# Scores and values on column tiles of their own, softmax groups of two heads and an earlier start, in a two-part attention decode kernel

## The chip, the cores and the metric

One core of one Trainium2 chip. The metric is the device time in microseconds (us), the median of the fast runs. The kernel before takes 1594.34 us (15 runs, 1592.09 to 1597.1).

## The reference

One decode step (one query token) of two attention blocks, their outputs side by side (shortened):

```python
# x (1,1,512); wq (512, 4096); wo (4096, 512); all bfloat16
def _A_ref(x, k_cache, v_cache, wq, wo):              # 32 heads, 32768 keys each
    q = (x @ wq) -> (1, 32, 1, 128)
    scores = einsum("bhqd,bhkd->bhqk", q, k_cache) * (128 ** -0.5)
    o = einsum("bhqk,bhkd->bhqd", softmax(scores), v_cache)
    return o.reshape(1, 1, 4096) @ wo
# _B_ref: the same with 8 KV heads for 32 query heads, and only the last 4096 keys
return concatenate([a, b], axis=-1)
```

Block A's caches are 32 x 32768 x 128 x 2 bytes, 268 MB each for K and V; with B and the weights, 570 MB have to be read. There is almost no reuse.

## The kernel before

A *chunk* is 1024 tokens of one KV head (1056 of them). TensorE (PE) transposes a chunk's K (called K below), multiplies it with the query (S, scores), and after the softmax multiplies the probabilities with V (PV). The code is shortened.

```python
NK_SLOTS = 5; NV_SLOTS = 8        # 1 MB load buffers for K and for V
NKT = 6                           # buffers for transposed K
A_TP_HEADS = [4, 4, 4, 4, 4, 4, 4, 2, 1, 1]   # heads of A in each softmax group

def pe_KX(i):                     # K: eight 128x128 transposes, then a copy by ACT or DVE into ktr
    for j in range(8):
        last = nc.tensor.transpose(out=bank[:, j*128:(j+1)*128], in_=kbuf[:, slot, off: off + DH],
                                   identity=ident_bf[:, :])

def pe_S(i):                      # S: the query sits in one of 128 columns, the others are zero;
    stat = qz[:, start_col: start_col + 128]        # so each chunk adds its own row of scores
    for b in range(2):
        last = nc.tensor.matmul(sps[:, b*512:(b+1)*512], lhsT=stat, rhs=ktr[:, kslot, b*512:(b+1)*512],
                                start=first_of_tp, stop=last_of_tp)

def pe_PV(i):                     # PV: lhsT is one column (A) or four (B) of the transposed probabilities
    for j in range(8):
        last = nc.tensor.matmul(obank[0:qg.rep, 0:DH], lhsT=pts[:, j*128 + r0: j*128 + r0 + qg.rep],
                                rhs=vbuf[:, slot, off: off + DH], start=..., stop=...)

while ...:                        # one round
    for _b in range(3): pe_KX(...)        # 24 K
    for _b in range(3): pe_S(...)         #  6 S; after the end of a softmax group the next S stands three rounds later
    for _b in range(3): pe_PV(...)        # 24 PV, of the group before
```

All PE completions that others wait for count up one semaphore. A load of V is issued when the PVs of the load eight before it are done. The V of a head is used only when the probabilities of its whole softmax group exist.

Of the kernel before, what the change touches and what calls it, by code (L numbers as in the profile page):

```python
# [9 lines left out]
DH = 128  # L10
# [3 lines left out]
NV_SLOTS = 8  # L14
NKT = 6
# [75 lines left out]
def build(nc, A_x, A_k, A_v, A_wq, A_wo, B_x, B_k, B_v, B_wq, B_wo, out):  # L91
# [26 lines left out]
    A_TP_HEADS = [4, 4, 4, 4, 4, 4, 4, 2, 1, 1]  # L118
# [65 lines left out]
    WZA = 256 - 1  # L184
    WZB = 256 - rep_B
# [5 lines left out]
    NPT = 3  # L191
    p_sb = nc.alloc_sbuf_tensor("p_sb", [128, NPT, SC_TOK], dt.bfloat16)
# [29 lines left out]
    sem_ld_sync = nc.alloc_semaphore("ld_sync")  # L222
    sem_ld_pool = nc.alloc_semaphore("ld_pool")
    sem_woA = nc.alloc_semaphore("woA")
    sem_woB = nc.alloc_semaphore("woB")
    sem_out = nc.alloc_semaphore("outdma")

# [14 lines left out]
    n_ld_sync = 3  # L242
    def ld_sync():
        with nc.allow_non_contiguous_dma(reason="tiny x transpose load"):
            nc.sync.dma_start(xtA[:, :], A_x[0, 0, :].rearrange("(kt p) -> p kt", p=128)).then_inc(sem_ld_sync, 16)
            nc.sync.dma_start(xtB[:, :], B_x[0, 0, :].rearrange("(kt p) -> p kt", p=128)).then_inc(sem_ld_sync, 16)
        nc.sync.dma_start(wbuf[:, 0:KT * H_A * DH].rearrange("p (kt n) -> p kt n", kt=KT),
                          A_wq.rearrange("(kt p) n -> p kt n", p=128)).then_inc(sem_ld_sync, 16)
        return None
    sch.add(SYNC, ld_sync)  # L250
    wqB_view = vbuf[:, 0:4, :].rearrange("p a b -> p (a b)")[:, 0:KT * Hq_B * DH].rearrange("p (kt n) -> p kt n", kt=KT)
    def ld_pool():
        nc.gpsimd.dma_start(wqB_view, B_wq.rearrange("(kt p) n -> p kt n", p=128)).then_inc(sem_ld_pool, 16)
        return None
    sch.add(POOL, ld_pool)
    wqA_view = wbuf[:, 0:KT * H_A * DH].rearrange("p (kt n) -> p kt n", kt=KT)

    def qphase():
        last = None
        for part, H, wq_view, xt, off in [('A', H_A, wqA_view, xtA, QCA_OFF), ('B', Hq_B, wqB_view, xtB, QCB_OFF)]:  # L260
            for h in range(H):
                for kt in range(KT):
                    last = nc.tensor.matmul(misc[:, off + h: off + h + 1],  # L263
                                            lhsT=wq_view[:, kt, h * DH:(h + 1) * DH],
                                            rhs=xt[:, kt:kt + 1],
                                            start=(kt == 0), stop=(kt == KT - 1))
        return last
    toks = {}
    def schedule_qphase():
        toks['qph'] = sch.add(PE, qphase, deps=[t_const, (sem_ld_sync, 16 * n_ld_sync), (sem_ld_pool, 16)], stamp=True)  # L270

    def qz_build():
        nc.scalar.activation(out=qzA[:, :, WZA - 128: WZA - 127].rearrange("p h o -> p (h o)"),
                             in_=misc[:, QCA_OFF: QCA_OFF + H_A],
                             func=ACT.Copy, scale=scale)
        return nc.scalar.activation(out=qzB[:, :, WZB - 128: WZB - 128 + rep_B],  # L276
                                    in_=misc[:, QCB_OFF: QCB_OFF + Hq_B].rearrange("p (g j) -> p g j", j=rep_B),
                                    func=ACT.Copy, scale=scale)
    def schedule_qz():
        toks['qz'] = sch.add(ACTE, qz_build, deps=[t_const, toks['qph']], stamp=True)  # L280
# [58 lines left out]
    def schedule_wo_and_v():  # L339
        sch.add(POOL, woA_dma, deps=[toks['qph']])  # L340
        for j in range(min(NV_SLOTS, NDMA)):
            v_dma_issue(j, extra_deps=[toks['qph']])
# [191 lines left out]
    def act_evac_o(qg, hd_tok):  # L534
        def body():
            if qg.part == 'A':
                outv = oA[0:1, qg.kv_head, :]
            else:
                outv = oB[0:qg.rep, qg.kv_head, :]
            return nc.scalar.activation(out=outv, in_=ops[qg.gidx % 2][0:qg.rep, 0:DH], func=ACT.Copy)  # L540
        ev_tok[qg.gidx] = sch.add(ACTE, body, deps=[hd_tok], stamp=True)

    def pe_S(i):
# [4 lines left out]
        last_of_tp = (i == tp_last_sc[t])  # L548
        if qg.part == 'A':
# [5 lines left out]
        start_col = (W0 - 128) - r0  # L555
        assert 0 <= start_col and start_col + 128 <= W0, (start_col, W0, r0)
        stat = qz[:, start_col: start_col + 128]
        kslot = i % NKT
        deps = [kt_evac_tok[i]]
        if i == 0:  # L560
            deps.append(toks['qz'])
# [3 lines left out]
        def body():  # L565
            last = None
            for b in range(2):
                last = nc.tensor.matmul(sps[:, b * 512:(b + 1) * 512], lhsT=stat,  # L568
                                        rhs=ktr[:, kslot, b * 512:(b + 1) * 512],
                                        start=first_of_tp, stop=last_of_tp)  # L570
# [8 lines left out]
    def pe_PV(i):  # L579
# [24 lines left out]
        def body():  # L604
            last = None
            for j in range(jn):
                off = tile_off(c, j)
                last = nc.tensor.matmul(obank[0:qg.rep, 0:DH],  # L608
# [60 lines left out]
    while s_next < NSC or pv_queue or hooks or kx_next < NSC:  # L669
# [14 lines left out]
        for _b in range(BATCH):  # L684
# [13 lines left out]
    def pe_final1():  # L698
        for qg in qgroups:
            if qg.part == 'A':  # L700
                h = qg.heads[0]
                nc.tensor.matmul(misc[:, OT_OFF + h: OT_OFF + h + 1], lhsT=oA[0:1, qg.kv_head, :],
                                 rhs=ident_bf[0:1, 0:1], start=True, stop=True)
            else:
                nc.tensor.matmul(misc[:, OT_OFF + qg.heads[0]: OT_OFF + qg.heads[0] + qg.rep],
                                 lhsT=oB[0:qg.rep, qg.kv_head, :],
                                 rhs=ident_bf[0:qg.rep, 0:qg.rep], start=True, stop=True)
# [71 lines left out]
```

## Time and profile before

| | before |
|---|---|
| time | 1594.34 us |
| chain of work that ended last | 90% PE |
| round of 24 K, 6 S, 24 PV | 4.17 us |
| read while in steady state | 374 GB/s |

The prediction below shows the chain, the waits and the timeline. Here are three more lines of the page of the kernel before: busy time of each engine, the gigabytes per second in 40 equal slices of the span, and the loads of K (count, size, median us from issue to landing).

```profile
PE 1496.3 (94%) x19197; PEld 1145.8 (72%) x19524; DVE 396.0 (25%) x607; ACT 549.8 (35%) x616; POOL 12.4 (1%) x14
...
GB/s 369 372 359 365 306 226 371 385 373 383 349 375 382 374 377 349 378 386 373 338 376 374 385 373 350 378 379 384 340 384 376 377 383 339 388 375 387 290 401 174
...
kbuf<-in_A_k_cache_dram SPq DMA_DIRECT2D x256, 1024.0 KB, 9.4
```

Most slices show 340 to 388 GB/s, and nothing holds this rate down except that PE frees buffers no faster. A K load lands 9.4 us after its issue.

### The profile page before, as it was taken

The numbers are of one execution on the slowest core, as the hardware profiler recorded it, in microseconds if no ns is written. First come the engines' busy times: TensorE is split into PE (matmuls) and PEld (weight loads), VectorE is DVE, ScalarE is ACT, GpSimd is POOL, SyncE is SP. The second block draws the span as 40 slices with busy tenths as digits, with TensorE's granted clock in tenths as the row PEclk, the third lists the DMA queues.
The fourth block names the chain that finished last, engine by engine and source line by source line (L and its number), as shares of the span: only waits on it lengthen the run. The fifth ranks groups of instructions, "written<-read, shape, count | busy, mean of one in ns | idle before, by whom it ended". The sixth has DMA issues, their size and how long they took to land.

```text
span 1591.9 us, 40850 instructions
## 1 busy us (share of the span) xinstructions
PE 1496.3 (94%) x19197; PEld 1145.8 (72%) x19524; DVE 396.0 (25%) x607; ACT 549.8 (35%) x616; POOL 12.4 (1%) x14
## 2 busy tenths in 40 slices
PE   2789999999999999999999999999999999999977
PEld 2567767777777777777777777777777777777865
DVE  0223332222222232222222222222322222222200
ACT  1334543333333333333333333333333333333200
POOL 2000000000000000000000000000000000000000
PEclk8899999999999999999999999999999999999999
DMA  9999869999999999999899999999999999999794
GB/s 369 372 359 365 306 226 371 385 373 383 349 375 382 374 377 349 378 386 373 338 376 374 385 373 350 378 379 384 340 384 376 377 383 339 388 375 387 290 401 174
DMA packets 151050, 573.10 MB, mean 360 GB/s; under 512 B 9569, under 2 KB 13665, under 8 KB 149858
## 3 DMA queue, kind: packets, MB, share of 16 engines
q1 hardware_dynamic: 77506, 285.23, 46.7%
q10 hardware_dynamic: 71808, 276.84, 46.0%
q0 software_dynamic: 1568, 8.39, 1.3%
q8 instruction: 154, 2.52, 0.6%
q14 instruction: 14, 0.11, 0.0%
HBM read 570.43 MB, written 0.00 MB: 358 GB/s over the span
## 4 chain that ended last, share of the span: by engine, by line
PE 90%; DMA 6%; issue 2%; ACT 1%; POOL 1%; ACTq 0%; DVE 0%; POOLq 0%
PE tb L403 31%; PE ops L608 29%; PE sps L568 27%; DMA vbuf<-in_A_v_cache_dram 3%; DMA vbuf<-in_B_wq_dram 1%; DMA kbuf<-in_A_k_cache_dram 1%; ACT p_sb L473 1%; PE sps L732 1%; PE misc L263 0%; POOL qzA L238 0%; ACTq L321 0%; PE tb L489 0%; PE misc L515 0%; PE misc L435 0%; PE misc L457 0%
## 5 line engine op out<-in xcount | busy, mean ns | idle before, releaser
L418 ACT ACTIVATE ktr<-tb 128x1024 bf16<-128x1024 bf16 x528 | 521.8, 1021 | 884.8 <-PE tb L403 872.3
L421 DVE COPY ktr<-tb 128x1024 bf16<-128x1024 bf16 x528 | 365.2, 692 | 1042.6 <-PE tb L403 1042.4
L403 PE MATMUL tb<-ident_bf,kbuf 128*128 128x128 bf16 x8448 | 538.5, 220 | 35.4 <-DMA kbuf<-in_B_k_cache_dram 26.3
L608 PEld LDWEIGHTS ops<-vbuf,pt_sb 128*1 128x1 bf16 (+1 forms) x8448 | 462.8, 84 | 149.8 <-issue 130.0
L403 PEld LDWEIGHTS tb<-ident_bf,kbuf 128*128 128x128 bf16 x8448 | 480.7, 98 | 85.4 <-issue 33.8
L608 PE MATMUL ops<-vbuf,pt_sb 128*1 128x128 bf16 (+1 forms) x8448 | 526.1, 219 | 15.6 <-DMA vbuf<-in_A_v_cache_dram 13.4
L568 PE MATMUL sps<-ktr,qzA 128*128 128x512 bf16 x1727 | 431.9, 381 | 33.9 <-ACT p_sb L473 17.4
L568 PEld LDWEIGHTS sps<-ktr,qzA 128*128 128x128 bf16 x2048 | 186.0, 98 | 178.1 <-ACT p_sb L473 16.6
L540 ACT ACTIVATE oA<-ops 1x128 bf16<-1x128 f32 x32 | 8.5, 266 | 107.5 <-PE ops L608 84.9
L568 PE MATMUL sps<-ktr,qzB 128*128 128x512 bf16 x58 | 16.4, 422 | 1.3 <-ACT qzB L276 0.9
L473 ACT ACTIVATE p_sb<-sps,nmcol 128x512 bf16<-128x512 f32 (+2 forms) x22 | 14.7, 669 | 7.9 <-DVE nmcol L464 7.9
L714 DVE RECIPROCAL recip<-ops 128x64 f32<-128x64 f32 x1 | 0.6, 557 | 67.6 <-PE ops L708 67.6
L429 DVE TENSOR_REDUCE rmax<-sps 128x1 f32<-128x1024 f32 (+2 forms) x11 | 13.4, 1220 | 8.6 <-PE sps L568 8.6
L498 DVE COPY pt_sb<-tb 128x1024 bf16<-128x1024 bf16 (+2 forms) x11 | 6.5, 595 | 25.8 <-PE tb L489 25.8
L568 PEld LDWEIGHTS sps<-ktr,qzB 128*128 128x128 bf16 x64 | 6.3, 107 | 6.8 <-issue 1.6
L489 PEld LDWEIGHTS tb<-ident_bf,p_sb 128*128 128x128 bf16 (+2 forms) x88 | 6.2, 110 | 3.0 <-issue 1.3
L732 PE MATMUL sps<-kbuf,ots 128*1 128x512 bf16 x32 | 7.1, 379 | 0.9 <-DVE ots L716 0.9
L489 PE MATMUL tb<-ident_bf,p_sb 128*128 128x128 bf16 (+2 forms) x88 | 7.3, 234 | 0.0
L732 PE MATMUL sps<-wbuf,ots 128*1 128x512 bf16 x32 | 7.1, 379 | 0.0
L540 ACT ACTIVATE oB<-ops 4x128 bf16<-4x128 f32 x8 | 2.1, 266 | 14.2 <-PE ops L608 14.2
L238 POOL MEMSET qzA<- 128x8160 bf16 x1 | 6.9, 6897 | 0.0
L740 ACT ACTIVATE fin_sb<-sps 1x1024 bf16<-1x1024 f32 x1 | 1.0, 1012 | 16.4 <-PE sps L732 16.4
(41 smaller groups left out, 62.7 us busy)
## 6 DMA issues: line engine op xcount, KB each, us to landing
kbuf<-in_A_k_cache_dram SPq DMA_DIRECT2D x256, 1024.0 KB, 9.4
vbuf<-in_A_v_cache_dram ACTq DMA_DIRECT2D x256, 1024.0 KB, 9.2
kbuf<-in_B_k_cache_dram SPq DMA_DIRECT2D x8, 1024.0 KB, 22.2
vbuf<-in_B_v_cache_dram ACTq DMA_DIRECT2D x8, 1024.0 KB, 27.0
wbuf<-in_A_wq_dram SPq DMA_DIRECT2D x1, 4096.0 KB, 13.0
vbuf<-in_B_wq_dram POOLq DMA_DIRECT2D x1, 4096.0 KB, 19.7
wbuf<-in_A_wo_dram POOLq DMA_DIRECT2D x1, 4096.0 KB, 36.3
kbuf<-in_B_wo_dram SPq DMA_DIRECT2D x1, 4096.0 KB, 39.7
```

The costliest lines, as they stand in the source:

```text
L238: sch.add(POOL, lambda: nc.gpsimd.memset(qzA[:], 0.0))
L403: last = nc.tensor.transpose(out=bank[:, j * 128:(j + 1) * 128], in_=kbuf[:, slot, off: off + DH], identity=ident_bf[:, :])
L418: etok = sch.add(ACTE, lambda: nc.scalar.activation(out=ktr[:, kslot, :], in_=bank[:, :], func=ACT.Copy), deps=edeps, stamp=True)
L421: etok = sch.add(DVE, lambda: nc.vector.tensor_copy(out=ktr[:, kslot, :], in_=bank[:, :]), deps=edeps, stamp=True)
L429: return nc.vector.reduce_max(out=rmax[0:rows, t:t + 1], in_=sps[0:rows, :], axis=AXIS.X)
L473: last = nc.scalar.activation(out=p_sb[0:rows, slot, b * 512:(b + 1) * 512], in_=sps[0:rows, b * 512:(b + 1) * 512], func=ACT.Exp, bias=nm ...
L489: last = nc.tensor.transpose(out=bank[:, j * 128: j * 128 + rows], in_=p_sb[0:rows, slot, j * 128:(j + 1) * 128], identity=ident_bf[0:rows ...
L498: return nc.vector.tensor_copy(out=outv, in_=inv)
L540: return nc.scalar.activation(out=outv, in_=ops[qg.gidx % 2][0:qg.rep, 0:DH], func=ACT.Copy)
L568: last = nc.tensor.matmul(sps[:, b * 512:(b + 1) * 512], lhsT=stat, rhs=ktr[:, kslot, b * 512:(b + 1) * 512], start=first_of_tp, stop=last ...
L608: last = nc.tensor.matmul(obank[0:qg.rep, 0:DH], lhsT=pts[:, j * 128 + r0: j * 128 + r0 + qg.rep], rhs=vbuf[:, slot, off: off + DH], start ...
L732: last = nc.tensor.matmul(sps[0:1, base + nb * 512: base + nb * 512 + w], lhsT=ots[:, h: h + 1], rhs=wo_view[:, hl, nb * 512: nb * 512 + w ...
```

## The change

The intent: S and PV each use few columns of the 128x128 array, so put them on different *column tiles*, so that they can run at the same time. S goes from all 128 columns to the 32-column tile of its band of rows; PV moves from columns 0 on to columns 64 on. So that A's bands do not meet PV's tile, A's softmax groups shrink from four heads (128 rows) to two (64 rows). Besides that: more buffers for transposed K, one less for V, B's query projection first and A's in the seam between B and A. The order of K, S and PV in the program stays.

```diff
-NV_SLOTS = 8
-NKT = 6
+NV_SLOTS = 7
+NKT = 10
-    A_TP_HEADS = [4, 4, 4, 4, 4, 4, 4, 2, 1, 1]
+    A_TP_HEADS = [2] * 15 + [1, 1]
-    WZA = 256 - 1
-    WZB = 256 - rep_B
+    SBAND = 32
+    WZA = 2 * SBAND - 1
+    WZB = 2 * SBAND - rep_B
+    PVP = 64
 ...                                   # start: B's weights first, both on the ACT queue
+    sch.add(ACTE, ld_B)
+    sch.add(ACTE, ld_A)
 ...                                   # A's projection when the first A scores are due
+            if qg.part == 'A' and 'qphA' not in toks:
+                schedule_qphase_A(t - 1)
 ...                                   # pe_S
-        stat = qz[:, start_col: start_col + 128]
+        stat = qz[:, start_col: start_col + SBAND]
-                last = nc.tensor.matmul(sps[:, b * 512:(b + 1) * 512], lhsT=stat,
+                last = nc.tensor.matmul(sps[SBAND * band: SBAND * (band + 1), b * 512:(b + 1) * 512], lhsT=stat,
                                         rhs=ktr[:, kslot, b * 512:(b + 1) * 512],
-                                        start=first_of_tp, stop=last_of_tp)
+                                        start=first_of_band, stop=last_of_band,
+                                        tile_position=(0, SBAND * band))
 ...                                   # pe_PV, and the copies of its result
-                last = nc.tensor.matmul(obank[0:qg.rep, 0:DH],
+                last = nc.tensor.matmul(obank[PVP:PVP + qg.rep, 0:DH],
```

More of the change, by code (lines that the diff above doesn't have):

```diff
@@ L221, in build @@
     vsem = [nc.alloc_semaphore(f"vslot{i}") for i in range(NV_SLOTS)]
-    sem_ld_sync = nc.alloc_semaphore("ld_sync")
-    sem_ld_pool = nc.alloc_semaphore("ld_pool")
+    sem_ld_A = nc.alloc_semaphore("ld_A")
+    sem_ld_B = nc.alloc_semaphore("ld_B")
     sem_woA = nc.alloc_semaphore("woA")
@@ L226, in build, with ld_B, ld_A @@
     sem_out = nc.alloc_semaphore("outdma")
+    wqB_view = vbuf[:, 0:4, :].rearrange("p a b -> p (a b)")[:, 0:KT * Hq_B * DH].rearrange("p (kt n) -> p kt n", kt=KT)
+    wqA_view = wbuf[:, 0:KT * H_A * DH].rearrange("p (kt n) -> p kt n", kt=KT)
+    def ld_B():
+        with nc.allow_non_contiguous_dma(reason="tiny x transpose load"):
+            nc.scalar.dma_start(xtB[:, :], B_x[0, 0, :].rearrange("(kt p) -> p kt", p=128)).then_inc(sem_ld_B, 16)
+        nc.scalar.dma_start(wqB_view, B_wq.rearrange("(kt p) n -> p kt n", p=128)).then_inc(sem_ld_B, 16)
+        return None
+    sch.add(ACTE, ld_B)
+    def ld_A():
+        with nc.allow_non_contiguous_dma(reason="tiny x transpose load"):
+            nc.scalar.dma_start(xtA[:, :], A_x[0, 0, :].rearrange("(kt p) -> p kt", p=128)).then_inc(sem_ld_A, 16)
+        nc.scalar.dma_start(wqA_view, A_wq.rearrange("(kt p) n -> p kt n", p=128)).then_inc(sem_ld_A, 16)
+        return None
+    sch.add(ACTE, ld_A)
     t_c = sch.add(POOL, lambda: nc.gpsimd.memset(ident_bf[:], 0.0), stamp=True)
@@ L240, in build, with qphase_part, body @@
     t_const = sch.add(POOL, lambda: nc.gpsimd.memset(tot[:], 1.0), stamp=True)
-    n_ld_sync = 3
-    def ld_sync():
-        with nc.allow_non_contiguous_dma(reason="tiny x transpose load"):
-            nc.sync.dma_start(xtA[:, :], A_x[0, 0, :].rearrange("(kt p) -> p kt", p=128)).then_inc(sem_ld_sync, 16)
-            nc.sync.dma_start(xtB[:, :], B_x[0, 0, :].rearrange("(kt p) -> p kt", p=128)).then_inc(sem_ld_sync, 16)
-        nc.sync.dma_start(wbuf[:, 0:KT * H_A * DH].rearrange("p (kt n) -> p kt n", kt=KT),
-                          A_wq.rearrange("(kt p) n -> p kt n", p=128)).then_inc(sem_ld_sync, 16)
-        return None
-    sch.add(SYNC, ld_sync)
-    wqB_view = vbuf[:, 0:4, :].rearrange("p a b -> p (a b)")[:, 0:KT * Hq_B * DH].rearrange("p (kt n) -> p kt n", kt=KT)
-    def ld_pool():
-        nc.gpsimd.dma_start(wqB_view, B_wq.rearrange("(kt p) n -> p kt n", p=128)).then_inc(sem_ld_pool, 16)
-        return None
-    sch.add(POOL, ld_pool)
-    wqA_view = wbuf[:, 0:KT * H_A * DH].rearrange("p (kt n) -> p kt n", kt=KT)
-    def qphase():
-        last = None
-        for part, H, wq_view, xt, off in [('A', H_A, wqA_view, xtA, QCA_OFF), ('B', Hq_B, wqB_view, xtB, QCB_OFF)]:
+    def qphase_part(part):
+        H, wq_view, xt, off, qbank = (H_A, wqA_view, xtA, 0, sps) if part == 'A' else (Hq_B, wqB_view, xtB, 0, ops[1])
+        def body():
+            last = None
             for h in range(H):
                 for kt in range(KT):
-                    last = nc.tensor.matmul(misc[:, off + h: off + h + 1],
+                    last = nc.tensor.matmul(qbank[:, off + h: off + h + 1],
                                             lhsT=wq_view[:, kt, h * DH:(h + 1) * DH],
@@ L266, in qphase, with schedule_qphase_A @@
                                             start=(kt == 0), stop=(kt == KT - 1))
-        return last
+            return last
+        return body
     toks = {}
     def schedule_qphase():
-        toks['qph'] = sch.add(PE, qphase, deps=[t_const, (sem_ld_sync, 16 * n_ld_sync), (sem_ld_pool, 16)], stamp=True)
-    def qz_build():
-        nc.scalar.activation(out=qzA[:, :, WZA - 128: WZA - 127].rearrange("p h o -> p (h o)"),
-                             in_=misc[:, QCA_OFF: QCA_OFF + H_A],
-                             func=ACT.Copy, scale=scale)
-        return nc.scalar.activation(out=qzB[:, :, WZB - 128: WZB - 128 + rep_B],
-                                    in_=misc[:, QCB_OFF: QCB_OFF + Hq_B].rearrange("p (g j) -> p g j", j=rep_B),
-                                    func=ACT.Copy, scale=scale)
+        toks['qphB'] = sch.add(PE, qphase_part('B'), deps=[t_const, (sem_ld_B, 32)], stamp=True)
+    def schedule_qphase_A(t_prev):
+        toks['qphA'] = sch.add(PE, qphase_part('A'), deps=[(sem_ld_A, 32), gettok('exp', t_prev), gettok('rmx', t_prev)],
+                               stamp=True)
+        toks['qzA'] = sch.add(ACTE, lambda: nc.scalar.activation(
+            out=qzA[:, :, SBAND - 1: SBAND].rearrange("p h o -> p (h o)"),
+            in_=sps[:, 0: H_A],
+            func=ACT.Copy, scale=scale), deps=[toks['qphA']], stamp=True)
+        sch.add(POOL, woA_dma, deps=[toks['qphA']])
     def schedule_qz():
-        toks['qz'] = sch.add(ACTE, qz_build, deps=[t_const, toks['qph']], stamp=True)
+        toks['qzB'] = sch.add(ACTE, lambda: nc.scalar.activation(
+            out=qzB[:, :, SBAND - rep_B: SBAND],
+            in_=ops[1][:, 0: Hq_B].rearrange("p (g j) -> p g j", j=rep_B),
+            func=ACT.Copy, scale=scale), deps=[t_const, toks['qphB']], stamp=True)
     V_ON_SCALAR = True
@@ L339, in schedule_wo_and_v @@
     def schedule_wo_and_v():
-        sch.add(POOL, woA_dma, deps=[toks['qph']])
         for j in range(min(NV_SLOTS, NDMA)):
-            v_dma_issue(j, extra_deps=[toks['qph']])
+            v_dma_issue(j, extra_deps=[toks['qphB']])
     tk = {}
@@ L536, in body @@
             if qg.part == 'A':
-                outv = oA[0:1, qg.kv_head, :]
+                outv = oA[PVP:PVP + 1, qg.kv_head, :]
             else:
-                outv = oB[0:qg.rep, qg.kv_head, :]
-            return nc.scalar.activation(out=outv, in_=ops[qg.gidx % 2][0:qg.rep, 0:DH], func=ACT.Copy)
+                outv = oB[PVP:PVP + qg.rep, qg.kv_head, :]
+            return nc.scalar.activation(out=outv, in_=ops[qg.gidx % 2][PVP:PVP + qg.rep, 0:DH], func=ACT.Copy)
         ev_tok[qg.gidx] = sch.add(ACTE, body, deps=[hd_tok], stamp=True)
+    sc_band = {}
+    band_first, band_last = {}, {}
+    for i2, (qg2, sc2) in enumerate(sclist):
+        r02 = qg2.row0 + sc2 * qg2.rep
+        bkey = (qg2.tp, r02 // SBAND)
+        sc_band[i2] = bkey
+        band_first.setdefault(bkey, i2)
+        band_last[bkey] = i2
+        assert r02 % SBAND + qg2.rep <= SBAND
     def pe_S(i):
@@ L548, in pe_S @@
         last_of_tp = (i == tp_last_sc[t])
+        bkey = sc_band[i]
+        band = bkey[1]
+        first_of_band = (band_first[bkey] == i)
+        last_of_band = (band_last[bkey] == i)
+        rb = r0 - SBAND * band
         if qg.part == 'A':
@@ L554, in pe_S @@
             W0 = WZB
-        start_col = (W0 - 128) - r0
-        assert 0 <= start_col and start_col + 128 <= W0, (start_col, W0, r0)
-        stat = qz[:, start_col: start_col + 128]
+        start_col = (SBAND - qg.rep) - rb
+        assert 0 <= start_col and start_col + SBAND <= W0, (start_col, W0, r0)
+        stat = qz[:, start_col: start_col + SBAND]
         kslot = i % NKT
         deps = [kt_evac_tok[i]]
-        if i == 0:
-            deps.append(toks['qz'])
+        if i == 0 or sclist[i - 1][0].part != qg.part:
+            if qg.part == 'A' and 'qphA' not in toks:
+                schedule_qphase_A(t - 1)
+            deps.append(toks['qzB'] if qg.part == 'B' else toks['qzA'])
         if first_of_tp:
@@ L683, in build @@
                 s_next += 1
-        for _b in range(BATCH):
+        npv = BATCH
+        for _b in range(npv):
             if pv_queue:
@@ L701, in pe_final1 @@
                 h = qg.heads[0]
-                nc.tensor.matmul(misc[:, OT_OFF + h: OT_OFF + h + 1], lhsT=oA[0:1, qg.kv_head, :],
-                                 rhs=ident_bf[0:1, 0:1], start=True, stop=True)
+                nc.tensor.matmul(misc[:, OT_OFF + h: OT_OFF + h + 1], lhsT=oA[PVP:PVP + 1, qg.kv_head, :],
+                                 rhs=ident_bf[PVP:PVP + 1, PVP:PVP + 1], start=True, stop=True)
             else:
                 nc.tensor.matmul(misc[:, OT_OFF + qg.heads[0]: OT_OFF + qg.heads[0] + qg.rep],
-                                 lhsT=oB[0:qg.rep, qg.kv_head, :],
-                                 rhs=ident_bf[0:qg.rep, 0:qg.rep], start=True, stop=True)
+                                 lhsT=oB[PVP:PVP + qg.rep, qg.kv_head, :],
+                                 rhs=ident_bf[PVP:PVP + qg.rep, PVP:PVP + qg.rep], start=True, stop=True)
         return nc.tensor.matmul(ops[0][:, 0:NH], lhsT=ones_f[0:1, 0:128], rhs=tot[0:1, 0:NH],
```

## The prediction

> **What bounds the kernel now.** I read the page's chain first, then the waits of TensorE (PE), then two pieces of the timeline, then the stretches by time. "Chunk" is 1024 tokens of one KV head; there are 1056. Each chunk costs PE eight 128x128 transposes of K (called K below, L403), two score matmuls of 512 columns (S, L568) and eight value matmuls of 128 columns (PV, L608). The program goes in rounds of three chunks: 24 K, 6 S, 24 PV. "Group" below is a softmax group: before, four A heads = 128 rows.
>
> The chain that ended last, from the page:
>
> ```profile
> PE 90%; DMA 6%; issue 2%; ACT 1%; POOL 1%; ACTq 0%; DVE 0%; POOLq 0%
> ```
>
> So PE is the chain. What PE waited for, in the waits view:
>
> ```profile
> PE tb L403 <- DMA kbuf<-in_B_k_cache_dram: 26.3, 3, 21.1
> PE sps L568 <- ACT p_sb L473: 17.4, 10, 2.1
> PE ops L608 <- DMA vbuf<-in_A_v_cache_dram: 13.4, 17, 1.4
> PE tb L403 <- ACT ktr L418: 7.1, 1, 7.1
> ```
>
> The first is the start, the third is the tail, the second is the softmax of the group ends. None belongs to the steady part. That is this (PE only; start, duration):
>
> ```profile
> 434.58 1.51 PE L403 MATMUL tb<-ident_bf,kbuf 128*128 128x128 bf16 x24
> 436.15 1.24 PE L568 MATMUL sps<-ktr,qzA 128*128 128x512 bf16 x5
> 437.32 1.50 PE L608 MATMUL ops<-vbuf,pt_sb 128*1 128x128 bf16 x24
> 438.76 1.51 PE L403 MATMUL tb<-ident_bf,kbuf 128*128 128x128 bf16 x24
> ```
>
> A round is 438.76 - 434.58 = 4.17 us (x5 is six with one record lost). Before the first A group has probabilities there are rounds without PV:
>
> ```profile
> 171.38 1.50 PE L403 MATMUL tb<-ident_bf,kbuf 128*128 128x128 bf16 x24
> 172.72 1.46 PE L568 MATMUL sps<-ktr,qzA 128*128 128x512 bf16 x6
> 174.01 1.50 PE L403 MATMUL tb<-ident_bf,kbuf 128*128 128x128 bf16 x24
> ```
>
> Such a round is 2.63 us. One matmul lasts 219 ns from entry to end, so 24 in 1.50 us start every (1500 - 219)/23 = 55.7 ns; six S in 1.46 us start every (1460 - 381)/5 = 216 ns. 24 x 55.7 + 6 x 216 = 2.63: K and S follow each other without a gap. A full round should then be 2.63 + 24 x 55.7 ns = 3.97, but is 4.17. The missing 0.20 us lies where PV begins and where it ends: S to PV is 437.32 less the start of the last S (about 437.01), 0.31 us where 0.216 would do; PV to K shows the other 0.1. So PE runs at its own pace all the time, and only those two seams are slack.
>
> DMA has some room. In the stretches view (time, busy times, clock, DMA share, GB/s):
>
> ```profile
> 140.00:217.00 77.00, 76.26 (x870) 56.48 (x882) 30.43 (x44) 42.66 (x44) 0.00 (x0) 1.00 0.91 322
> 240.00:580.00 340.00, 333.81 (x4295) 255.88 (x4372) 86.60 (x128) 122.66 (x132) 0.00 (x0) 1.00 0.98 374
> ```
>
> A round moves 3 x 0.524 = 1.573 MB, 377 GB/s at 4.17 us. In the tail, where only V comes, PE takes 32 matmuls per 1 MB load each 2.56 us:
>
> ```profile
> 1540.02 1.95 PE L608 MATMUL ops<-vbuf,pt_sb 128*1 128x128 bf16 x32 [0.61 <-DMA vbuf<-in_A_v_cache_dram]
> 1542.57 1.95 PE L608 MATMUL ops<-vbuf,pt_sb 128*1 128x128 bf16 x32 [0.60 <-DMA vbuf<-in_A_v_cache_dram]
> ```
>
> That is 1.049 MB / 2.56 us = 410 GB/s, which I take for the ceiling.
>
> **What the Trainium skill says.** (1) "TensorEngine Tiling (Array Packing)", Key Properties: changing the tiling mode, not just the tile, drains TensorE. The trace agrees: the built program has K and S in mode 128x128 and PV in 128x32, K to S shows no gap and the two mode changes about 0.1 us each. (2) The same section says that different tiles can load weights and multiply in parallel, and (3) "TensorE: Matmul & The Clock Gate", Part 3 (row/col tiling), gives 2.38 times for three column tiles and a start distance of about 4 ns, while matmuls stay in program order in start and end. Nothing in this trace shows it: all PV here sit on one tile. (4) "DMA: Bandwidth & Descriptors", Issuing engines are not separate DMA queues: all queues share the 16 engines, so moving loads to another queue changes order, not bandwidth.
>
> **The change, part by part.**
>
> Column tiles. S becomes 128x32 on the tile of its band of 32 rows (A groups now have two heads, 64 rows, tiles 0 and 32); PV moves to tile 64. The order K, S, PV stays. The mode changes now lie at K to S and PV to K; S to PV is only a change of tile. From the order of instructions of the two kernels: before 306 S-PV and 294 PV-K seams; after 344 K-S, 307 PV-K, and about 34 S-K or K-PV. At 0.095 (into 128x32) and 0.106 us (back): before 306 x 0.095 + 294 x 0.106 = 60 us, after 344 x 0.095 + 341 x 0.106 = 69 us. So +9 us by itself.
>
> The gain must come from overlap: the first PV may enter beside the last S, on another tile. S1 to S6 share one tile and starts are in order, so PV can pass only the last S: at most 216 - 4 = 212 ns for each of 326 S-PV seams, -69 us. The round becomes 3.96 us, 397 GB/s, still under 410.
>
> Softmax groups. A goes from ten groups (7 of four heads, 2, 1, 1) to 17 (15 of two, 1, 1). What one end costs, before: two K-to-K intervals of 4.01 and 6.31 us hold five chunks of work, so 10.32 - 5 x 1.391 = 3.4 us. In the timeline, from the last S (starts about 401.2) to the earliest second statistics matmul takes 0.42 + 1.23 (row maximum) + 0.05 + 0.42 + 0.28 + 0.03 + 0.21 = 2.6 us, then about 0.4 + 0.2 + 0.1 + 1.45 for copy and two exponentials. After, fewer PV and K are left to fill this (order: 24 PV, 8 K, 8 PV; before 24, 16, 16), because the PV queue is empty there. From the last S to the next K group I work out 5.3 (chain) + 1.3 (S) + 1.4 (transposes of p) = 8.0 us, with 3.8 us of useful work in it: 4.2 us each. Before: 8 x 3.4 + 6 (the first) + 1.7 (one end met a cold clock) = 35; after: 16 x 4.2 + 2 = 69. +34 us. More ktr buffers (10 for 6) let S use tiles transposed two rounds earlier, but PE waits for no evacuation in the steady part, so they gain nothing.
>
> Start. Before, the B weights land at 30 us, both projections end at 39.8, scores begin at 40.2. Now B's weights head the ACT queue and share with K: 4.2 MB at half of 410 GB/s, about 22 us, then one projection (3.6 us and a fetch of 2): scores at about 28. But ACT then issues seven V loads behind A's 4.2 MB on the same queue; before, it stood at this from 46.8 to 53.8 us; I expect it until 46 to 48. Then 11 rounds of 2.84 us: B's scores end near 77 instead of 84. A's projection (3.6 us and a copy) moves into the B-A seam, +4. Net -4.
>
> Tail. PV lags by one group: before, 115 chunks are left at the last softmax, and PE waits 16 us for V in all; now 59, of which seven slots (28 chunks) are loaded: about 8 waits of 0.6, 5 us. -11. B's output weights come later relative to the end: +3. One V slot less: nothing, V waits more than 25 us in its slot in the steady part.
>
> Sum: -69 + 9 + 34 - 4 - 11 + 3 = -38 us. The absolute sum (87 to the first A score, 1364 of PE work left, 67 seams, 68 ends, -69, 27 tail and end) gives 1544, and the same sum for the kernel before gives 1585 against 1592, so 1551 with the same shortfall. Between 1551 and 1556 I take 1553.
>
> **The rivals.** (A) No overlap: tiles are kept apart only in name, or PV's loads wait for the last S. For: nothing in this trace shows overlap. Against: the skill's packing figures, and that the extra ends would make no sense without it. Time 1594 + 31 = about 1622, 1.8% slower. (B) Part of it: if ends must also stay in order, a PV of 56 ns may start only so that it ends after the S of 216 ns; gain 56 ns per seam, -18 us: about 1603. (C) More: if each tile queues its own matmuls, the whole S block (1.3 us) runs beside PV; the round falls to 2.9 us and DMA becomes the bound at 1.573/410 = 3.84 us; 570.4 MB / 410 = 1391 plus start and end: 1460 to 1510. (D) The longer ends cool the clock each time (one cold end before cost 1.7 us): +16 x 1.5 = +24 on any of these.
>
> **Range and chances.** Full single overlap 57%, near 1553, with D partly in it up to 1577; no overlap 17%; part 13%; more 13%. Faster by over 2% is under 1562. So: predicted 1553 us, 8 in 10 between 1505 and 1615; faster 0.57, within 2% 0.37, slower 0.06.
>
> **What would show it.** Right: the round 3.96 us in the timeline, the first PV starting within some 10 ns of the last S, K to S gaps of 0.1 us, rounds without PV at 2.84, group ends costing about 4 us with PE waiting on the exponentials some 16 x 2 us, V waits under 10 us in the tail. Wrong: a round of 4.17 (A), 4.1 (B), or PE waiting for K or V in steady rounds with 400 GB/s (C); first S later than 30 us; K groups of 24 taking some 2.3 us instead of 1.5 after each end, as the one at 773 us before does (D).

## The result, and the profile after

| | before | after |
|---|---|---|
| time, median | 1594.34 us | 1464.48 us (8 runs, 1462.88 to 1466.84) |
| ratio, 95% interval | | 0.9189 (0.918 to 0.9198) |
| PE busy | 94% | 88% |
| round where PE has its data | 4.17 us | 3.33 us |
| 240 to 580 us: read | 374 GB/s | 408 GB/s |

A ratio here is the mean time of one kernel's fast runs over the mean of the other's fast runs of the same rounds, so it is not quite the ratio of the medians. The result is correct. The change gives 8.1%, 130 us, where 41 us were predicted; it is below the predicted range.

The page of the kernel after: busy times, rate in 40 slices, the chain by engine, the K loads.

```profile
PE 1285.1 (88%) x19622; PEld 1058.0 (72%) x19622; DVE 408.9 (28%) x656; ACT 566.4 (39%) x644; POOL 5.3 (0%) x13
...
GB/s 368 409 301 408 307 409 408 408 409 408 407 408 408 406 408 405 409 408 402 407 408 408 389 408 405 389 408 408 408 398 408 406 408 408 400 408 408 396 387 113
...
PE 52%; DMA 41%; ACT 3%; DVE 2%; ACTq 1%; issue 1%
...
kbuf<-in_A_k_cache_dram SPq DMA_DIRECT2D x256, 1024.0 KB, 20.3
```

Four readings say the same. PE is on the chain for 52% instead of 90%, and DMA has 41% of it instead of 6%. The rate sits at 408 GB/s in nearly every slice, where it varied between 340 and 388: a flat top means a ceiling. A K load now takes 20.3 us instead of 9.4: loads wait in line. And PE, whose work was 94% of a longer span, has idle time. The bound moved from PE to DMA.

What PE waited for (total us, times, longest), in the waits view of the kernel after:

```profile
PE tb L410 <- DMA kbuf<-in_A_k_cache_dram: 75.9, 74, 2.4
PE sps L592 <- ACT p_sb L480: 32.3, 16, 2.2
...
PE ops L633 <- DMA vbuf<-in_A_v_cache_dram: 14.4, 11, 1.4
```

The first line is new: before, PE waited 2.0 us in all for A's K, now 75.9 us in 74 waits. The second is the softmax at the end of 16 groups.

Now the timeline of PE in the kernel after (start, duration, then operation; "x4" is four matmuls in a row). One round that waits for K, then one round that has its data:

```profile
396.29 0.61 PE L410 MATMUL tb<-ident_bf,kbuf 128*128 128x128 bf16 x8 [1.15 <-DMA kbuf<-in_A_k_cache_dram]
...
432.56 1.51 PE L410 MATMUL tb<-ident_bf,kbuf 128*128 128x128 bf16 x24
434.00 0.82 PE L592 MATMUL sps<-ktr,qzA 128*32 128x512 bf16 x3
434.45 0.38 PE L633 MATMUL ops<-vbuf,pt_sb 128*1 128x128 bf16 x4
434.66 0.38 PE L592 MATMUL sps<-ktr,qzA 128*32 128x512 bf16 x1
...
435.12 0.83 PE L633 MATMUL ops<-vbuf,pt_sb 128*1 128x128 bf16 x12
435.88 1.51 PE L410 MATMUL tb<-ident_bf,kbuf 128*128 128x128 bf16 x24
```

This is the surprise. The program has six S and then 24 PV. PE starts three S, then four PV, then the fourth S, and so on: of 24 PV, 12 have started before the last S. The first PV starts at 434.45, beside the third S, and before the fourth, fifth and sixth S, which stand earlier in the program. From K to K the round takes 435.88 - 432.56 = 3.32 us, where 4.17 us were needed.

In the view of stretches (time, busy us of PE, PEld, DVE, ACT and POOL with counts, clock, DMA share, GB/s), over 340 us in the middle:

```profile
240.00:580.00 340.00, 308.73 (x4747) 256.69 (x4745) 99.93 (x160) 136.92 (x154) 0.00 (x0) 0.97 1.03 408
```

A round reads 1.573 MB, so at 408 GB/s a round takes 3.86 us on average. PE would do it in 3.33.

**The ledger of missing bytes.** For a kernel at the DMA's ceiling it pays to read the rate row as an account. 573.1 MB in all at 408 GB/s take 1405 us. A slice with x GB/s loses (408 - x)/408 of its length, and these losses are all that a further change can win. For the kernel after (slices of 36.6 us): 3.5 us in the first two slices, 18.5 in the next six (301 and 307 are the two holes), 9.4 in the next 31, 26.4 in the last: 57.9 us, and 1405 + 58 is the span of 1462 us. The kernel before loses 114 us in those 31 middle slices, this one 9.4.

### The profile page after: what moved, and what is told of

Read it like the earlier page. It is cut to its first block, busy times and chain, and to the rows that moved or that the text cites. A ratio compares the mean times of both kernels' runs of the same rounds, so it can differ in the third digit from the quotient of the medians.

```text
span 1462.4 us, 41465 instructions
## 1 busy us (share of the span) xinstructions
PE 1285.1 (88%) x19622; PEld 1058.0 (72%) x19622; DVE 408.9 (28%) x656; ACT 566.4 (39%) x644; POOL 5.3 (0%) x13
## 3 DMA queue, kind: packets, MB, share of 16 engines
q0 software_dynamic: 1040, 4.19, 0.8%
## 4 chain that ended last, share of the span: by engine, by line
PE 52%; DMA 41%; ACT 3%; DVE 2%; ACTq 1%; issue 1%
DMA kbuf<-in_A_k_cache_dram 37%; PE tb L410 21%; PE ops L633 14%; PE sps L592 13%; DMA vbuf<-in_A_v_cache_dram 3%; ACT p_sb L480 2%; DMA vbuf<-in_B_wq_dram 1%; DVE rmax L436 1%; PE sps L758 1%; ACTq L329 1%; ACT ktr L425 1%; DVE ktr L428 1%; PE tb L496 1%; PE misc L442 0%; PE misc L522 0%
## 5 line engine op out<-in xcount | busy, mean ns | idle before, releaser
L425 ACT ACTIVATE ktr<-tb 128x1024 bf16<-128x1024 bf16 x528 | 527.2, 1022 | 782.4 <-PE tb L410 762.6
L410 PE MATMUL tb<-ident_bf,kbuf 128*128 128x128 bf16 x8448 | 557.2, 222 | 104.8 <-DMA kbuf<-in_A_k_cache_dram 75.9
L633 PE MATMUL ops<-vbuf,pt_sb 128*1 128x128 bf16 (+1 forms) x8448 | 530.9, 219 | 15.8 <-DMA vbuf<-in_A_v_cache_dram 14.4
L592 PE MATMUL sps<-ktr,qzA 128*32 128x512 bf16 x2048 | 513.3, 390 | 32.7 <-ACT p_sb L480 32.3
L592 PEld LDWEIGHTS sps<-ktr,qzA 128*32 128x32 bf16 x2048 | 170.2, 98 | 157.4 <-ACT p_sb L480 33.8
L480 ACT ACTIVATE p_sb<-sps,nmcol 64x512 bf16<-64x512 f32 (+2 forms) x36 | 24.3, 676 | 4.2 <-DVE nmcol L471 3.8
L436 DVE TENSOR_REDUCE rmax<-sps 64x1 f32<-64x1024 f32 (+2 forms) x18 | 21.7, 1208 | 4.4 <-PE sps L592 4.4
L505 DVE COPY pt_sb<-tb 128x512 bf16<-128x512 bf16 (+2 forms) x18 | 7.6, 425 | 51.3 <-PE tb L496 51.3
L592 PE MATMUL sps<-ktr,qzB 128*32 128x512 bf16 x64 | 16.7, 415 | 0.0
L496 PEld LDWEIGHTS tb<-ident_bf,p_sb 64*128 64x128 bf16 (+2 forms) x144 | 7.3, 114 | 12.5 <-issue 12.3
L442 PE MATMUL misc<-ident_f,rmax 64*1 64x64 f32 (+2 forms) x36 | 4.8, 214 | 10.7 <-DVE rmax L436 10.7
L515 DVE TENSOR_TENSOR sumcol<-rsum 64x1 f32<-64x1 f32 (+2 forms) x18 | 2.7, 152 | 34.1 <-ACT p_sb L480 34.1
L496 PE MATMUL tb<-ident_bf,p_sb 64*128 64x64 bf16 (+2 forms) x144 | 9.8, 222 | 0.0
## 6 DMA issues: line engine op xcount, KB each, us to landing
kbuf<-in_A_k_cache_dram SPq DMA_DIRECT2D x256, 1024.0 KB, 20.3
vbuf<-in_A_v_cache_dram ACTq DMA_DIRECT2D x256, 1024.0 KB, 20.3
kbuf<-in_B_wo_dram SPq DMA_DIRECT2D x1, 4096.0 KB, 50.2
```

The source lines that it names most:

```text
L410: last = nc.tensor.transpose(out=bank[:, j * 128:(j + 1) * 128], in_=kbuf[:, slot, off: off + DH], identity=ident_bf[:, :])
L425: etok = sch.add(ACTE, lambda: nc.scalar.activation(out=ktr[:, kslot, :], in_=bank[:, :], func=ACT.Copy), deps=edeps, stamp=True)
L436: return nc.vector.reduce_max(out=rmax[0:rows, t:t + 1], in_=sps[0:rows, :], axis=AXIS.X)
L480: last = nc.scalar.activation(out=p_sb[0:rows, slot, b * 512:(b + 1) * 512], in_=sps[0:rows, b * 512:(b + 1) * 512], func=ACT.Exp, bias=nm ...
L496: last = nc.tensor.transpose(out=bank[:, j * 128: j * 128 + rows], in_=p_sb[0:rows, slot, j * 128:(j + 1) * 128], identity=ident_bf[0:rows ...
L505: return nc.vector.tensor_copy(out=outv, in_=inv)
```

## The experiments

Every run also ran the kernel before on the same chip; it was at 1591.98 to 1595.47 us in all of them. The theory after the result: (T1) matmuls of different column tiles pass each other within a window, so four S of a round run beside PV, not one, and the kernel then stands at the DMA's ceiling. The rivals: (T2) the gain is from the buffers, the start and the groups, and the tiles matter little; (T3) the gain comes from narrower S (32 columns to load), not from the overlap.

### 1. S over all columns again

```diff
-    SBAND = 32
+    SBAND = 128
-NKT = 10
+NKT = 6
```

The first form of it kept ten buffers for transposed K. With the wide query tiles they no longer fitted into the on-chip memory, and nine did not fit either, so it has six, as before the change.

> The changed kernel with the score matmuls put back into the full 128x128 mode (ktr buffers 6, as before, for space); start, softmax groups, V slots, PV on tile 64 stay changed. Theory O (the gain is PV matmuls entering beside S on another column tile of the same mode): no overlap is left, PE round back at 4.17 us, total 1600 to 1630 (the sum of the prediction without its overlap term, 1616), so 1 to 2 percent slower than the kernel before. Rival R (the gain comes from the start, the smaller groups and the shorter tail): stays near 1465 to 1520.

Measured: 1630.84 us (1630.13 to 1631.47), ratio 1.0235 (1.0218 to 1.0252). Its timeline (one S record of six is lost):

```profile
433.19 1.51 PE L410 MATMUL tb<-ident_bf,kbuf 128*128 128x128 bf16 x24
434.75 1.24 PE L592 MATMUL sps<-ktr,qzA 128*128 128x512 bf16 x5
435.93 1.50 PE L633 MATMUL ops<-vbuf,pt_sb 128*1 128x128 bf16 x24
```

All PV start after all S, and the round is 4.17 us again (the next K group starts at 437.36). The time lies just above the expected 1600 to 1630. So the whole of the gain hangs on the column tiles, and everything else in the change together (with six buffers for ten) costs 37 us while PE is the bound. T2 falls.

### 2. S over 64 columns

```diff
-    SBAND = 32
+    SBAND = 64
-NKT = 10
+NKT = 9
```

S then uses columns 0 to 63 and PV columns 64 on: disjoint, but tiles of two sizes.

> S in tiles of 64 columns (mode 128x64, tile 0 for the A heads), PV still on tile 64 in mode 128x32 (9 ktr buffers). The columns of S and PV are still disjoint, but S to PV is now a change of mode. If a change of mode drains PE whatever the columns: like full_s, round 4.17 to 4.27 us, 1600 to 1640. If disjoint columns are enough: 1465.

Measured, one look: 1659.37 us, a single run, so its state is not known. It lies above the expected range. From its timeline:

```profile
433.99 1.48 PE L592 MATMUL sps<-ktr,qzA 128*64 128x512 bf16 x6
435.40 1.50 PE L633 MATMUL ops<-vbuf,pt_sb 128*1 128x128 bf16 x24
```

The last S starts at about 433.99 + 5 x 0.22 = 435.09, the first PV 0.31 us later: no overlap. The round is 4.29 us: 438.28 - 433.99 from the first S of one round to the first S of the next. That is 0.12 us more than with two sizes, for one more change of size per round. So it is not enough that the columns are disjoint; both have to be tiles of the same size. It also speaks against T3: a narrower S alone gains nothing.

### 3. PV back on tile 0

```diff
-    PVP = 64
+    PVP = 0
```

Now the first head of a group (band 0) shares its tile with PV, the second (band 1) does not. S stays narrow for both.

> PV on tile 0, all else as changed. S of the first head of a group is on tile 0 too, of the second on tile 32: theory O expects the two kinds of round in turn within each group, 4.17 us (same tile, nothing to overlap) for the first 32 chunks and 3.33 for the next; per group 44.5 + 35.5 + 4.3 = 84.3 us of PE against 82.2 of DMA, so some 2 us more per group: about 1490 (1475 to 1520). Rival R: 1465.

Measured: 1502.47 us (1501.69 to 1503.14), ratio 0.943 (0.9416 to 0.9445). Its timeline where one head follows the other:

```profile
457.23 1.50 PE L633 MATMUL ops<-vbuf,pt_sb 128*1 128x128 bf16 x24
458.67 1.51 PE L410 MATMUL tb<-ident_bf,kbuf 128*128 128x128 bf16 x24
...
461.42 1.50 PE L633 MATMUL ops<-vbuf,pt_sb 128*1 128x128 bf16 x24
...
471.83 0.39 PE L633 MATMUL ops<-vbuf,pt_sb 128*1 128x128 bf16 x4
```

On one tile the 24 PV stand in one piece, and the round is 461.42 - 457.23 = 4.19 us; on two tiles they are split into fours as in the kernel after, and the round is 3.32 us (K groups at 469.94 and 473.26). Same sizes, same program order, one kernel: only the tile differs. T3 falls, T1 stands.

### 4. Groups of four heads

```diff
-    A_TP_HEADS = [2] * 15 + [1, 1]
+    A_TP_HEADS = [4, 4, 4, 4, 4, 4, 4, 2, 1, 1]
```

Fewer group ends for PE; but the third head of a group has PV's tile.

> The changed kernel with the softmax groups of the kernel before (four heads, 10 groups). S runs over tiles 0, 32, 64, 96, PV sits on 64: theory O expects rounds of 3.33 us with every third quarter of a group at 4.17. PE has room (154 us a group of 128 chunks, DMA 164), so DMA stays the bound; but 32 rounds without PV instead of 11 before the first A probabilities (V slots full, K alone some 276 GB/s) lose about 10 us of DMA time more: 1470 to 1485. Rival R, which holds the groups responsible for much of the gain: over 1520.

Measured: 1485.91 us (1484.63 to 1487.14), ratio 0.9327 (0.9313 to 0.934): 21 us slower than the kernel after, and just above the expected 1470 to 1485. The rounds on PV's tile do take 4.19 us, yet the middle of the kernel stays at 408 GB/s: the load buffers ride over them. The rate row and one stretch of it:

```profile
GB/s 368 409 297 408 335 259 322 408 409 408 407 408 409 408 408 408 409 408 406 404 409 408 397 409 404 408 399 401 405 409 408 398 408 392 409 408 397 386 403 104
```

```profile
180.00:200.00 20.00, 20.00 (x215) 13.00 (x213) 7.24 (x12) 10.43 (x11) 0.00 (x0) 1.00 0.78 273
```

Slices 3 to 8 lose 38.1 us here against 18.5 in the kernel after. That is 19.6 of the 20.4 us between the two spans. The stretch tells why: until the first A group of four heads has its probabilities no V is used, all V buffers are full, and only K is read, as fast as PE transposes and scores it. A round without PV took 2.85 us in the kernel after, for 0.786 MB of K, which is 276 GB/s; 273 is what the stretch shows. Groups of two end this stretch after half as many chunks. So the groups that were made for the tiles gain their 21 us at the DMA.

### 5 to 7. Half of each load

These three read only half of each 1 MB load and use it twice. The result is wrong (relative error 0.583). It shows PE's own pace without the DMA.

```diff
-            src = qg.k_src[qg.tok0 + t0: qg.tok0 + t0 + dtok, :]
-            nb = dtok // BLK_TOK
+            src = qg.k_src[qg.tok0 + t0: qg.tok0 + t0 + BLK_TOK, :]
+            nb = 1
 ...                         # the same for V
-        b = c // 2
+        b = 0
```

The kernel after with half loads:

> Wrong result on purpose: every K and V load brings half of its tokens (0.5 MB instead of 1 MB) and PE reads that half twice, so all PE, ACT and DVE work stays and the DMA load of K and V halves. If the changed kernel is now bound by DMA and its PE alone would need 3.33 us a round: waits for K vanish and the time falls to about 1335 (1310 to 1370). If it is still bound by PE: 1450 to 1465.

The kernel before with half loads:

> The same halved loads in the kernel before. It was bound by PE with 14 us of slack on K: only the V waits of the tail (16 us) and the K waits of the first phase (10) go; 1560 to 1575, rounds still 4.17 us.

The kernel after with half loads, and PV put between the S chunks in the program:

```diff
                 s_next += 1
-        npv = BATCH
-        for _b in range(npv):
             if pv_queue:
                 pe_PV(pv_queue.pop(0))
```

> after_half with S and PV chunks alternating in the program (two S, eight PV, two S, ...) instead of six S, then 24 PV. In the changed kernel PV starts only beside the third of six S, as if about three S could wait at their tile while later work passes. If that is a limit on how far PE looks ahead, alternating lifts it: S and PV side by side throughout, round 1.34 + 0.2 + 1.34 = 2.9 us instead of 3.33, total some 140 us under after_half: about 1195. If PE shares something else between the tiles: no change from after_half.

Measured, one look each (single runs, so their state is not known): 1322.42, 1560.25 and 1206.73 us. The chain of the kernel after with half loads:

```profile
PE 92%; ACT 3%; DVE 2%; DMA 2%; issue 1%; ACTq 0%
```

No wait for A's K or V is left, and the rounds are again 3.33 us. The kernel before gains only 32 us from half loads: it was bound by PE, as predicted. With half loads the whole change is worth 238 us (1560.25 to 1322.42), with whole loads 130: so some 108 us of what it gives PE never reach the time of the kernel after. As an estimate, 326 seams x 0.84 us less the 34 us that the prediction charged for the extra group ends are 240, close to these 238; the estimate leaves out the start and the tail.

The third one's timeline:

```profile
433.41 0.39 PE L592 MATMUL sps<-ktr,qzA 128*32 128x512 bf16 x1
433.42 0.38 PE L633 MATMUL ops<-vbuf,pt_sb 128*1 128x128 bf16 x4
...
434.50 0.38 PE L592 MATMUL sps<-ktr,qzA 128*32 128x512 bf16 x1
434.53 0.39 PE L633 MATMUL ops<-vbuf,pt_sb 128*1 128x128 bf16 x4
```

With S and PV close together in the program, PV starts beside the first S, every S has its four PV, and the round is 434.85 - 431.97 = 2.88 us (from K to K). In the kernel after, the program has all S first, and PV starts beside the third of six. So there is a window, and how the program orders the two decides how much of them overlaps.

### 8 and 9. The window measured in the final projection

Near the end of both kernels stand 64 matmuls of 512 columns on one tile (32 for B, 32 for A; 14 us before, 15 us after), a place without softmax and loads. Both experiments put B's on tile 32 and A's on tile 0, copy the two halves of the result with two engines, and write them with two DMAs.

```diff
-                    last = nc.tensor.matmul(sps[0:1, base + nb * 512: ...
+            prow = 0 if part == 'A' else 32
+            last = nc.tensor.matmul(sps[prow:prow + 1, base: base + DOUT],
 # final_pairs:  order = [(p, i) for i in range(H_A) for p in ('A', 'B')]
 # final_blocks: order = [(p, i) for p in ('B', 'A') for i in range(H_A)]
```

A and B in turn:

> The changed kernel; the output projection at the end (64 matmuls of 512 columns, one tile, 15 us after the last V) put on two tiles, A heads on 0 and B heads on 32, alternating A, B in the program; the final copy split between ACT and DVE. If two tiles stream at once, 64 matmuls take 32 x 0.216 = 7 us: 7 to 8 us off the changed kernel, 1457 (8.6 percent under before instead of 8.1). If the overlap of S and PV needs something else: no change.

First all B, then all A:

> The same two tiles, but all 32 B matmuls first, then all 32 A. If PE can pass about three waiting matmuls of another tile, A enters beside the third last B: the projection takes 13.2 us, the whole under 1.5 us less than the changed kernel (split copy included). If tiles take whole queues: as final_pairs.

Measured: in turn 1458.29 us (1456.7 to 1459.96), ratio 0.9151 (0.9139 to 0.9164); in blocks 1463.16 us (1462.02 to 1463.81), ratio 0.9183 (0.9169 to 0.9197), as good as the kernel after. The timeline of the blocks (kbuf holds B's weights, wbuf A's):

```profile
1444.43 6.42 PE L754 MATMUL sps<-kbuf,ots 128*1 128x512 bf16 x29 [0.91 <-DVE ots L742]
1450.48 0.38 PE L754 MATMUL sps<-wbuf,ots 128*1 128x512 bf16 x1
1450.69 0.38 PE L754 MATMUL sps<-kbuf,ots 128*1 128x512 bf16 x1
```

The 29th B starts at 1444.43 + 6.42 - 0.38 = 1450.47; the first A starts at 1450.48 beside it, while three B have still to start. In the rounds the first PV also started when three S had still to start. So in both places a matmul passed exactly three that wait for the other tile. The whole trace of the kernel after refines this. In 291 of its 306 rounds with all records, the first PV starts while three S have still to start. In the other 15, S changes from tile 0 to tile 32 within the round. There four S have still to start, by program order one for tile 0 and three for tile 32, and the round takes 2.90 us. So three looks like a limit for each tile, not for all tiles together. Whether three is a count of matmuls, or of matmuls with their weight loads, no run tells.

### 10. The column tiles alone

The kernel before with SBAND = 32, PVP = 64 and nothing else of the change: groups of four, the old start, the old buffers.

> The kernel before with the column tiles alone: S in bands of 32 on tiles 0 to 96, PV on tile 64. Old start, old groups of four heads, 6 ktr buffers, 8 V slots. Theory O: nearly the whole gain is here; like the run with groups of four (1486), which has the new start and buffers too: 1480 to 1500. If the new start or the buffers carry part of the gain: over 1510.

Measured: 1480.46 us (1480.22 to 1483.77), ratio 0.9293 (0.9278 to 0.9309). So the tiles alone give 114 us of the 130. It differs from the groups of four in the fourth experiment by the start and the buffers only, and is 5 us *faster*, on another chip (the ratios, 0.9293 and 0.9327, say the same). The ledger shows where. The rate row of this run:

```profile
GB/s 373 351 393 408 308 274 324 408 408 407 408 407 408 408 408 408 408 408 408 402 409 408 397 407 397 408 408 397 400 408 408 403 408 398 408 407 400 365 401 139
```

Its first two slices lose 8.3 us, against 3.5 with the new start in run 4; but its third loses only 1.4, against 10.1 in run 4 (297 GB/s, the seam in which A's projection waits). So in the ledger the new start costs 3.9 us net. In the last slice run 4 loses 3.2 us more, and 3.0 less in the slices between. No run tests start and buffers one by one.

### 11. Groups of one head

On top of the projection in turn: each A head is its own softmax group, which needs small row buffers reused in turn.

```diff
-    A_TP_HEADS = [2] * 15 + [1, 1]
+    A_TP_HEADS = [1] * 32
-    grp = nc.alloc_sbuf_tensor("grp", [128, NTP, 128], dt.float32)
+    grp = nc.alloc_sbuf_tensor("grp", [128, 2, 128], dt.float32)     # brow too, indexed t % 2
```

> final_pairs (1458) with A softmax groups of one head each (32 of them; the two small statistics tiles become a ring of two, for space). DMA is the bound, and its largest hole is the stretch at 160 to 180 us, where V slots are full and no A probabilities exist yet; with one-head groups PV always has 32 chunks beside 32 chunks of S, so the hole goes: 10 us less, 1448 (1442 to 1456). PE needs 10.67 x 3.33 + 4.3 = 39.8 us a group against 41.1 of DMA, so it is tight: if the 16 added group ends cost more than that, no gain or a loss.

Measured: 1446.76 us (1445.68 to 1447.82), ratio 0.9075 (0.9062 to 0.9089). Its rate row:

```profile
GB/s 367 410 299 408 408 408 408 407 408 408 408 408 408 408 408 401 406 408 408 392 410 403 407 407 407 392 408 408 408 404 407 391 408 408 392 408 407 408 364 231
```

The second hole is gone (18.8 us lost in slices 3 to 8 of the kernel with the projection in turn, 9.7 here), and the last slice loses 15.7 instead of 20.6, since less V is left at the last softmax. Twice as many group ends cost nothing visible: in the 31 middle slices 11.5 us are lost instead of 9.5. So here too the prediction's +34 us for more ends does not show.

### 12. All together

On top of that: S and PV in turn in the program, A's projection in round 6 into free columns of another bank (before, it waited in the seam), eight V buffers, and a semaphore of its own for S.

```diff
-NV_SLOTS = 7
+NV_SLOTS = 8
-        H, ... = (H_A, wqA_view, xtA, 0, sps) if part == 'A' else ...
+        H, ... = (H_A, wqA_view, xtA, 448, misc) if part == 'A' else ...
+        if R == 6:
+            schedule_qphase_A()
-        tok = sch.add(PE, body, deps=deps, stamp=True)
+        tok = sch.add(PE, body, deps=deps, stamp=True, on='scores')
```

> ones, with S and PV chunks alternating in the program (PE round 2.88 in inter_half, so PE 35 us a group against 41 of DMA), the A projection moved from the first softmax end into the B phase, 8 V slots, and the completions of S counted on a semaphore of their own (matmuls of other tiles finish ahead of them). The hole at 80 to 90 us shrinks by about 4 us: 1440 (1434 to 1450). If DMA was not the bound of ones but PE, the gain over ones is larger than 8 us.

Measured: 1440.42 us (1439.22 to 1440.86), ratio 0.9035 (0.9021 to 0.9048), correct. It beats both kernels. Its rate row:

```profile
GB/s 367 400 361 409 408 408 408 408 408 408 408 407 409 408 407 404 408 399 408 401 409 405 407 396 408 407 401 409 408 395 408 408 408 399 409 408 393 407 367 237
```

The hole at the seam (299 in the third slice) has become 361. By the ledger 34.1 us are missing, of which 15.1 in the last slice. PE's round of 2.88 us is worth almost nothing here: the 31 middle slices lose 10.7 us instead of the 11.5 of run 11, so it can have given 0.8 us at most. The DMA is the bound.

## Why the prediction was wrong

**What bounds the kernel before** was read rightly. PE sets its pace: half loads took off 32 us of 1592. The prediction's sums hold but for three slips, too small to matter: rival A's 1594 + 31 is 1625, not 1622; the parts shown of a group end's chain add up to 4.8 us, not 5.3; the start's parts (-7 and +4) give -3, not -4.

**The step that failed** is: "S1 to S6 share one tile and starts are in order, so PV can pass only the last S: at most 216 - 4 = 212 ns for each of 326 S-PV seams, -69 us." Starts are not in order across tiles. PV passes up to three waiting S, so four S of each round run beside PV, not one. By the prediction's own term that is 4 x 0.212 = 0.85 us for each round, and 4.17 - 3.33 = 0.84 us was measured. The failed assumption was taken over from the Trainium skill ("TensorE: Matmul & The Clock Gate", Part 3), though the trace of the kernel before, with all PV on one tile, could not show it. Four times the size also carried it past the limit that the prediction itself had worked out: 3.96 us per round was to stay under the DMA, 3.33 us does not.

**The rivals.** A (no overlap) is what runs 1 and 2 show for tiles of different sizes: 1622 was worked out for it, 1631 measured in run 1. B (a PV may start only so late that it ends after the S) is refuted by the timeline: the first PV starts at 434.45 us, 0.64 us before the last S at 435.09, and the round is 3.33 us, not 4.1. The trace gives modelled ends; completions are still counted in program order (closing list). C (each tile has its own order; then DMA is the bound, 1460 to 1510) is what happened, and got 13%. Its round of 2.9 us is not the usual one of this change but that of S and PV in turn (2.88). D (the clock cools at group ends) came true in the trace: around the end at 405.82 us the granted clock was 0.65 (405 to 409 us), and the six S there take 2.38 us instead of 1.47. With the DMA as the bound it costs little: the 31 middle slices lose 9.4 us in all, whatever the cause.

**The size of the DMA's limit** was right: 410 GB/s taken from the tail, 408 measured over 340 us.

**The mode changes.** K to S now shows 1.44 us from the first K to the first S, of which 24 x 0.0557 = 1.34 are transposes: 0.1 us, as predicted, and rounds without PV took 2.85 us (predicted 2.84).

**Group ends, +34.** The sign was wrong for the kernel as it came out. PE does wait 16 times, 32.3 us in all, as predicted (16 x 2 us). But at the DMA's ceiling this idle time is filled from the other side: loads go on and the rate stays at 408. What groups do there is to set how long V buffers stand full before the first probabilities, and smaller groups gain 21 us (run 4). The term was PE's account applied to a kernel that DMA bounds. Where PE is the bound (run 1) the sign is right: 1631 us measured, 1616 worked out for that run.

**Start, -4.** First scores at 28.9 us (predicted about 28), the ACT queue was held until 46.5 (46 to 48), and B's scores ended near 76 (77). The mechanism was right for PE. What the sum did not hold is the hole in the rate at the seam, where A's projection waits for B's last softmax: 301 GB/s in that slice, 9.6 us lost; by run 10 it outweighs what the early start gains, and run 12 makes it smaller.

**Tail, -11 + 3.** V waits in the tail were put at about 5 us and below 10; they are 14.4. B's output weights share the rate with the last V loads: they took 50.2 us to land, from 1391 to 1441 us, and in that time the V loads landed 3.3 us apart, against 2.56 in the tail before.

## What to carry to other kernels

Before a change makes one engine faster, work out at which pace the next one becomes the bound, and price every other term of the change (group ends, buffers, start) for that bound, not for the old one; once the DMA is at its ceiling, the row of rates read as missing bytes tells what is left and where. For matmuls on different column tiles, use tiles of the same size and put the two kinds in turn in the program.

## What the Trainium skill lacked or had wrong

- "TensorE: Matmul & The Clock Gate", Part 3 (row/col tiling), says that matmuls stay in program order in start and in end, and "PSUM — Partial Sum Buffer", Engine vs sequencer instructions, says that they start and complete in program order. Across column tiles the order of starts does not hold here: a PV at 434.45 us starts before three S that stand earlier in the program (the next one at 434.66), and an A matmul of the final projection starts beside the 29th of 32 B.
- The first of these pages concludes that one increment on the last matmul is sound. The trace of the kernel after agrees: completions are counted in program order, although starts are not. In 79 cases a PV that PE's semaphore counts starts ahead of an S that stands earlier. Near 95 us, for example, that S lasts from 95.262 to 95.641 us and is counted at 95.655; the PV lasts from 95.009 to 95.228 and is counted only at 95.747. In all 79 the S is counted 14 or 15 ns after its end, the PV at least 56 ns after that end, and nothing is counted within the 20 ns after the PV's own end, where the kernel before counts all its 264 PV. So run 12's own semaphore for S was not needed for this; no run leaves it out of run 12.
- No page gives the depth of this passing: three waiting matmuls of one tile in both places where it could be counted; a round of 3.33 us with S first and 2.88 us in turn.
- "TensorEngine Tiling (Array Packing)", Key Properties, says that a change of mode drains TensorE, without a size: about 0.1 us each here (4.29 us for a round with one change more than 4.17). Run 2 agrees with it: disjoint columns in two modes did not overlap.
- "DMA: Bandwidth & Descriptors", Where 436 GB/s comes from, says that about 358 GB/s bind for loads from HBM. That sentence does not hold for one core alone: here 408 GB/s were held for 340 us. The same page has higher rates for a single core in its other sections, so the skill does not lack the figure; this one sentence leaves out the condition.
